# Attention's first two pairs in the written order, and the split parts of x stored a step earlier

## The chip, the cores and the metric

The kernel runs on one core of one Trainium2 chip. The metric is the device time in microseconds; before the change it is 2102.82 us, the median of 3 runs (2101.58 to 2103.69).

## What is computed

Three layers follow each other, all in float32:

```python
# attention: q, k, v of shape (4, 8, 576, 64)
scores = where(causal, -1e9, q @ k.T / 8)
local = softmax(scores) @ v
q_p = phi(q)                        # elu(q) + 1
mem_out = (q_p @ M_prev) / (q_p @ z_prev + 1e-6)
x = g * mem_out + (1 - g) * local   # g = sigmoid(beta), one per head
# x becomes (2304, 512)
x = (silu(x @ w_gate) * (x @ w_val)) @ w_out          # d_ff 1536
# routed layer, 8 experts, F 1024, all of them for every token
P = exp(logits - max); 8 times: rows, then columns to a sum of one, then * N / E
out = sum over e of P[:, e] * (relu(x @ w1[e]) @ w2[e])
```

## The kernel before

Products of float32 numbers are made of a high and a low part of each operand (names ending in H and L, or two halves of one tile), in three products; the low part is the difference between the number and its rounded high part. ACT makes the high part by a cast, DVE or POOL the low one by a subtraction.

**Attention** takes the 32 heads as 16 pairs. A pair's work is cut into steps by generators, and each has a letter: L loads a pair and makes its operands QH, QL, KH and KL (L301), Q prepares phi (ph, pz and nb, L333), S and E are scores (L396), N and K the factors from the row sums and the scaling on POOL (L372), V and Y the transposes (L474), W and U the products with the values (L515), C early weight work (L593), and X are filler matmuls into a spare PSUM tile (`po<-mask`), which give no result. Scores go by row blocks 4 (576 columns, in two halves), 3 (448), 2 (320, with block 0) and 1 (192). For each, PE writes a PSUM tile ps (there are two), DVE takes the row maximum (nm4 down to nm0), and ACT the exponent into P4 down to P1 and E0, with its sum. Then DVE turns the sums and the gate factors gs into factors, POOL scales P in place, PE transposes it into pt (three PSUM buffers), ACT and DVE copy it out (T, F, Z), and PE multiplies by the values into po, which is added up in xacc.

The strings BEGIN, ORDER and END (L39 to 57) give the order in which the steps are written: BEGIN the first two pairs, ORDER each later pair, shifted by the numbers in LAG, END what is left. The class `Ordered` (L79) hands every instruction to the scheduler with the demand to keep program order while `self.steady` is true. Before the change this is so only behind the steps of BEGIN and the first round of ORDER; the scheduler places what these steps issue freely on each engine. `gates` (L274) makes from beta eb, g1 and the ten small copies gs, and the high and low part of the routing weights (wgs). FIRST is the number of the step at which its second half is issued.

**The gated layer** (moe1) runs over 2304 tokens and **the routed layer** (moe2) over units of experts. The finished x is also needed as sums and differences of its blocks, in high and low parts, which are kept in DRAM. `parts_of` (L718) makes these: for each of a list of blocks a cast into a tile xl (two buffers), the difference, and a store xp<-xl. It is a generator, moved on by one step between pieces of the layers' own work; at each step it first does what is left from the step before, so a cast, its difference and its store fall into three following steps. Pairs 0 and 1 of token groups go through it in moe1 and pair 2 there too, with stores on SP's queue; pair 3 and the rest go through it in the first unit of moe2, with stores on ACT's queue. `logits` (L683) makes the routing logits in chunks and is moved on in the same way beside moe2's first unit; for a chunk of two tiles it has one step less in each of four rounds than for a larger one.

Of the kernel before, what the change touches and what calls it, by code (L numbers as in the profile page):

```python
# [42 lines left out]
ORDER = """  # L43
# [4 lines left out]


BEGIN = """  # L50
    L0 L0 Q0 X33 L1 L0 L0 S0 L2 X5 Q0 S0 S0 X5 S0 X7 X9 Q0 Q0 L1 Q1 L1 K0 X7 L1 S0 X5 Q1 N0 Q0 X7 X7 Q1
    V0 S0 S1 Q1 S1 S1 N0 V0 V0 V0 V0 V0 S1 S1 L2 Q1 L2 V0 W0 N0 W0 V0 V0 V0 S1 L2 V0 N1 N1 N1 W0
"""
END = """
# [1 line left out]
    U-1 U-1 U-1 U-1 U-1 U-1 U-1  # L56
"""

FIRST = 6

COPIES = "AAAAVVAVAVA"

# [1 line left out]
def schedule(n):  # L64

    steps = lambda text, base: [(s[0], base + int(s[1:])) for s in text.split()]
    middle = [(s, i + LAG[s]) for i in range(2, n) for s in ORDER.split() if i + LAG[s] < n]
    return steps(BEGIN, 0) + middle + steps(END, n)


def joined(steps, *counts):

    for n in counts:
        for _ in range(n):
            next(steps)
        yield
# [58 lines left out]
def f32(ap):  # L135
    return ap.bitcast(F32)
# [26 lines left out]
class Kernel:  # L163
# [34 lines left out]
    def attention(self, after=None):  # L198
        tc = self.tc
        nc = self.nc = Ordered(tc.nc, tc, lambda: self.steady)  # L200
        with ExitStack() as st, ExitStack() as first:
            pool = lambda n, b, to=st, **k: to.enter_context(tc.tile_pool(name=n, bufs=b, reuse_waits="tile", **k))

            self.s1, self.s2 = (pool(f"s{n}", n, first, side="right") for n in (1, 2))
            self.a1, self.a2, self.a3, self.a4 = (pool(f"a{n}", n) for n in (1, 2, 3, 4))
            self.pss = pool("pss", 2, space=PSUM)
            self.pst = pool("pst", 3, space=PSUM)
            self.pso = pool("pso", 1, space=PSUM)
            a1 = self.a1
            self.identb = self.s1.tile([P, P], BF16, name="identb")  # L210
            nc.vector.tensor_copy(self.identb, self.ident)

            self.mask = self.s1.tile([P, P], BF16, name="mask")
            nc.gpsimd.memset(self.mask, 0.0)
            nc.gpsimd.affine_select(
                out=self.mask, in_=self.mask, compare_op=ALU.is_ge, fill=MASKED,
                base=0, pattern=[[1, P]], channel_multiplier=-1,
            )
            self.mask0 = self.s1.tile([P, 2, 64], BF16, name="mask0")
            nc.gpsimd.memset(self.mask0, 0.0)  # L220
            for j in range(2):
                self.masked = nc.vector.tensor_copy(self.mask0[0:64, j], self.mask[0:64, 0:64])
            busy = self.pso.tile([P, 512], F32, name="po")

            self.P0 = []
            for n in range(2):
                t = a1.tile([P, 2, D], F32, name=f"P0{n}")
                nc.vector.memset(t, 0.0)
                self.P0.append(t)

            pairs = [(b, hp) for b in range(B) for hp in range(NP)][:self.n_pairs]
            n = len(pairs)
            live = [dict(b=b, hp=hp, P0=self.P0[hp % 2]) for b, hp in pairs]
            early = self.early()
            for p in live:
                p["steps"] = {
                    "L": self.load(p), "Q": self.prepare(p), "S": self.scores(p), "N": self.normalize(p),
                    "V": self.transposed(p), "W": self.values(p),
                }
                if p in live[:2]:  # L240
                    p["steps"]["S"] = joined(p["steps"]["S"], 2, 1, 2, 2, 2)
                if p is live[0]:
                    p["steps"]["V"] = joined(p["steps"]["V"], *10 * [1], 2)
                p["steps"].update({k: p["steps"][v] for k, v in SAME.items()})
                p["steps"]["C"] = early
            done = object()
            steps = schedule(n)
            for nth, (step, at) in enumerate(steps):
                self.steady = len(BEGIN.split()) + len(ORDER.split()) <= nth
                if nth == len(steps) - len(END.split()) and after:  # L250
                    self.ahead = self.load_units()
                    next(self.ahead)
                if nth == 1:
                    gates = self.gates()
                    next(gates)
                if nth == FIRST:
                    with tc.issue_after(self.low_q.ins):
                        next(gates, None)
                if step == "X":
                    for _ in range(at):  # L260
                        nc.tensor.matmul(busy[:, 0:P], self.mask, self.mask, start=True, stop=True)
                else:
                    next(live[at]["steps"][step], done)
            self.nc, self.steady = tc.nc, False
            first.close()
            if after:
                self.open_early(after)

                with tc.issue_after(self.last_exp.ins):
                    for _ in range(2):  # L270
                        next(self.ahead)
                    self.xs = self.split_x(*CHUNKS1[0])
# [410 lines left out]
    def logits(self, psum, name, pool, first, last, two=None):  # L683

        nc, m = self.nc, last - first
        pl = psum.tile([P, 512], F32, name=name)
        for k in range(NK):
            src = self.x[:, k, first * P:last * P]
            if two:
                t = [pool.tile([P, 512], F32R, name=two)[:, 0:m * P] for _ in range(2)]  # L690
            else:
                t = pool.tile([P, 2, 512], F32R, name="xl")
                t = [t[:, a, 0:m * P] for a in range(2)]
            nc.scalar.copy(t[0], src)
            if not two:
                yield
            nc.vector.tensor_sub(t[1], src, f32(t[0]))
            yield
            if two and m > 2:
                yield  # L700
            for a in range(2):
                nc.tensor.matmul(
                    pl[0:2 * E, 0:m * P], self.wgs[:, k], t[a], start=k + a == 0, stop=k == NK - 1 and a == 1
                )
        lt = pool.tile([P, 512], F32, name=two) if two else f32(pool.tile([P, 2, 512], F32R, name="xl")[:, 0])
        lt = lt[0:2 * E]
        nc.vector.tensor_copy(lt[:, 0:m * P], pl[0:2 * E, 0:m * P])
        yield
        yield
        pl = psum.tile([P, 512], F32, name=name)  # L710
        for t in range(m):
            nc.tensor.transpose(pl[:, t * 2 * E:(t + 1) * 2 * E], lt[:, t * P:(t + 1) * P], self.ident[0:2 * E, 0:2 * E])
        sums = self.Pw[:, first:last]
        pl = pl[:, 0:m * 2 * E].rearrange("p (t a e) -> p t a e", a=2, e=E)
        nc.vector.tensor_copy(sums, pl[:, :, 0])
        nc.vector.tensor_add(sums, sums, pl[:, :, 1])

    def parts_of(self, todo, queue):  # L718


        nc, rest = self.nc, []
        for src, dst in [*todo, (None, None), (None, None)]:
            nxt = []
            for what in rest:
                nxt += what()
            rest = nxt
            if src is not None:
                src = src()
                t = self.xl.tile([P, 2, 512], F32R, name="xl")
                hi, lo = (t[:, n].rearrange("p (k t) -> p k t", k=2) for n in range(2))  # L730
                nc.scalar.copy(hi, src)

                def low(src=src, dst=dst, t=t, hi=hi, lo=lo):
                    nc.vector.tensor_sub(lo, src, f32(hi))

                    def store():
                        queue.dma_start(dst, f32(t))
                        return []

                    return [store]  # L740

                rest.append(low)
            yield

    def parts(self, pair, queue):
# [22 lines left out]
    def moe1(self, last):  # L768
# [3 lines left out]
        with ExitStack() as st, ExitStack() as waiting, ExitStack() as banks:  # L772
# [61 lines left out]
            def more(c, logits):  # L834
                t0, n = CHUNKS1[c]
                if logits:
                    yield from self.logits(pgv, "p0", self.xl, t0 // P, (t0 + n) // P)
                yield from self.parts(c, nc.sync)
# [798 lines left out]
```

## Time and profile before

| | |
|---|---|
| median of 3 runs | 2102.82 us (2101.58 to 2103.69) |
| the profiled execution | 2105.53 us, span 2103.7 us |
| busy shares of the span | PE 98%, PEld 91%, DVE 82%, ACT 46%, POOL 25% |
| attention | from the start to about 230 us |

The profiled execution lies 2.7 us above the median. PE is TensorE's matmuls, PEld its weight loads, which overlap them. In attention nearly all instructions are recorded with one line, that of the wrapper (L93), so they are told apart by the tiles that they write and read; the names come without buffer numbers and without the block number, so P4 to P1 are all P, and the width tells them apart (576, 448, 320, 192).

### The profile page before, as it was taken

Reading aid. Unit: us, or ns where it says so; the run is one execution under the profiler, and the core shown is the slowest. Engines: PE = TensorE matmul, PEld = TensorE weight load, DVE = VectorE, ACT = ScalarE, POOL = GpSimd, SP = SyncE. Lnnn points to the kernel's source line nnn. Section 1 sums busy time; section 2 is a strip of 40 time slices with the busy share of each in tenths; the row PEclk is TensorE's granted clock in tenths of the full one; section 3 lists DMA queues with packets and bytes.
Section 4 is the critical chain, followed back from the end, with each engine's and each line's share of the span. In section 5 each row is a group of like instructions: output and inputs, shape, how many; then the busy total and the mean of one; then the engine's idle time right before and its main releaser. Section 6 shows DMA issues by size and latency. Waiting matters only on the chain.

```text
span 2103.7 us, 40585 instructions
## 1 busy us (share of the span) xinstructions
PE 2067.0 (98%) x15848; PEld 1907.4 (91%) x15848; DVE 1716.7 (82%) x3193; ACT 974.1 (46%) x1912; POOL 521.4 (25%) x458
## 2 busy tenths in 40 slices
PE   7999999999999999999999999999999999999999
PEld 5666787877889889999999999999999999999998
DVE  7899899675454668898888888888889888898887
ACT  6999543443333324444434444444444444444432
POOL 6888544000000042122121221212212122121210
PEclk9999999999999999999999999999999999999999
DMA  5342587476587747656566564665647656575564
GB/s 191 111 142 85 186 288 260 142 251 209 170 285 275 271 130 250 209 172 241 167 236 212 169 234 166 232 201 191 230 163 241 204 186 231 167 240 203 183 212 159
DMA packets 123359, 425.77 MB, mean 202 GB/s; under 512 B 13600, under 2 KB 13600, under 8 KB 120096
## 3 DMA queue, kind: packets, MB, share of 16 engines
q1 hardware_dynamic: 121728, 417.93, 59.3%
q10 hardware_dynamic: 1440, 5.24, 0.6%
q8 instruction: 126, 2.06, 0.4%
q14 instruction: 65, 0.53, 0.1%
HBM read 374.36 MB, written 48.76 MB: 201 GB/s over the span
## 4 chain that ended last, share of the span: by engine, by line
PE 71%; DVE 8%; DMA 4%; issue 1%; ACT 1%; SPq 0%; DVEq 0%; ACTq 0%
PE pu L1447 16%; PE pc L1284 15%; PE pq L1447 11%; PE pt L1284 10%; PE po L559 5%; PE pt L1370 4%; PE p L559 3%; PE pc L559 3%; PE pq L559 2%; DMA xr<-xp 2%; PE pt L559 2%; DMA xp<-xl 2%; DVE m L1300 2%; DVE xacc L1453 2%; DVE h L1269 1%; DVE h L1266 1%
## 5 line engine op out<-in xcount | busy, mean ns | idle before, releaser
L1447 PE MATMUL pu<-xl,h 128*128 128x256 f32 x3240 | 424.7, 278 | 2.6 <-DVE xacc L1453 2.1
L1447 PEld LDWEIGHTS pu<-xl,h 128*128 128x128 f32 x3240 | 393.0, 188 | 6.9 <-DVE xacc L1453 3.8
L1284 PE MATMUL pc<-xr,w 128*128 128x256 f32 x3048 | 390.5, 277 | 3.9 <-DMA xr<-xp 3.8
L1284 PEld LDWEIGHTS pc<-xr,w 128*128 128x128 f32 x3048 | 367.3, 188 | 7.2 <-issue 4.4
L1447 PE MATMUL pq<-xl,h 128*128 128x256 f32 x2430 | 317.1, 277 | 0.0
L1447 PEld LDWEIGHTS pq<-xl,h 128*128 128x128 f32 x2430 | 294.1, 188 | 0.4
L1284 PE MATMUL pt<-xr,w 128*128 128x256 f32 x2280 | 291.0, 277 | 0.0
L1268 ACT CAST h<-m 128x512 fp32r<-128x512 f32 (+1 forms) x345 | 190.4, 556 | 200.8 <-DVE m L1300 193.1
L1284 PEld LDWEIGHTS pt<-xr,w 128*128 128x128 f32 x2280 | 274.2, 188 | 0.7
L1453 DVE SCALAR_TENSOR_TENSOR xacc<-pu,Pw,xacc 128x256 f32<-128x256 f32 x540 | 237.1, 475 | 39.3 <-PE pu L1447 39.1
L1291 ACT COPY m<-pc 128x512 f32<-128x512 f32 x192 | 111.9, 583 | 249.6 <-PE pc L1284 245.7
L1453 DVE SCALAR_TENSOR_TENSOR xacc<-pq,Pw,xacc 128x256 f32<-128x256 f32 x405 | 177.5, 474 | 47.0 <-PE pq L1447 47.0
L1269 DVE TENSOR_TENSOR h<-m,h 128x512 fp32r<-128x512 f32 (+1 forms) x345 | 207.4, 625 | 1.5
L1189 POOL TENSOR_TENSOR ws<-raw 128x512 f32<-128x512 f32 x60 | 80.8, 1356 | 507.8 <-DMA raw<-w 165.6
L1265 ACT ACTIVATE h<-m 128x512 fp32r<-128x512 f32 x192 | 121.4, 633 | 172.3 <-DVE m L1296 164.9
L1300 DVE SCALAR_TENSOR_TENSOR m<-m 128x512 f32<-128x512 f32 x240 | 185.5, 773 | 14.2 <-ACT m L1327 10.6
L1296 DVE TENSOR_TENSOR m<-pt,m 128x512 f32<-128x512 f32 x192 | 131.3, 684 | 53.0 <-ACT m L1291 52.2
L559 PE MATMUL p<-xs,gw 128*128 128x512 f32 (+1 forms) x864 | 171.1, 355 | 3.4 <-ACT hf L796 1.3
L559 PEld LDWEIGHTS p<-xs,gw 128*128 128x128 f32 x864 | 142.3, 188 | 30.7 <-DVE hf L797 2.8
L1266 DVE SCALAR_TENSOR_TENSOR h<-m,h 128x512 fp32r<-128x512 f32 x192 | 150.3, 783 | 12.1 <-ACT h L1265 11.7
L1176 POOL TENSOR_TENSOR w<-raw,w 128x512 fp32r<-128x512 f32 x15 | 38.8, 2584 | 428.9 <-ACT w L1175 428.9
L559 PE MATMUL po<-h,ws 128*128 128x512 f32 x576 | 144.4, 391 | 0.2 <-DVE h L817 0.2
(232 smaller groups left out, 2956.9 us busy)
## 6 DMA issues: line engine op xcount, KB each, us to landing
xr<-xp SPq DMA_DIRECT2D x476, 512.0 KB, 4.2
raw<-w SPq DMA_DIRECT2D x64, 512.0 KB, 7.4
gw<-kg SPq DMA_DIRECT2D x24, 1024.0 KB, 7.0
graw<-gvo SPq DMA_DIRECT2D x36, 512.0 KB, 4.4
kg<-gw SPq DMA_DIRECT2D x24, 512.0 KB, 4.2
ws<-ko SPq DMA_DIRECT2D x24, 512.0 KB, 3.9
xp<-xl SPq DMA_DIRECT2D x21, 512.0 KB, 5.2
qk<-qkv SPq DMA_DIRECT2D x16, 640.0 KB, 5.2
```

The lines of the kernel that those rows point to most:

```text
L559: self.nc.tensor.matmul(out, lhs[a], rhs[b], start=start and n == 0, stop=stop and n == 2, skip_group_check=shared)
L1265: nc.scalar.activation(hi, src, AF.Relu)
L1266: self.later(1, lambda: nc.vector.scalar_tensor_tensor(lo, src, 0.0, f32(hi), op0=ALU.max, op1=ALU.subtract))
L1268: nc.scalar.copy(hi, src)
L1269: self.later(1, lambda: nc.vector.tensor_sub(lo, src, f32(hi)))
L1284: self.marks[3] = nc.tensor.matmul(out[:, j * HT:(j + 1) * HT], w[:, a, j, k], x[:, b, k], start=start and j + k + n == 0, stop=k + n == 3 ...
L1291: self.marks[1] = nc.scalar.copy(t, src)
L1296: nc.vector.tensor_add(t, a, b)
L1300: relu = lambda out, a, b, op: nc.vector.scalar_tensor_tensor(out, a, 0.0, b, op0=ALU.max, op1=op)
L1370: nc.tensor.matmul(ph[:, j * HT:(j + 1) * HT], w[:, b, j, k], x[:, c, k], start=j + a + k + m == 0, stop=a + k + m == 4, skip_group_check= ...
L1447: nc.tensor.matmul(po[:, c], h[a][:, x, j, c * P:(c + 1) * P], w2[b][:, y, j], start=start and c + j + n == 0, stop=j + n == 3, skip_group ...
L1453: self.marks[2] = nc.vector.scalar_tensor_tensor(acc, po[:, c], self.Pw[:, at, e:e + 1], acc, op0=ALU.mult, op1=ALU.add)
```

## The change

Four things are edited. All steps of attention are kept in program order (`self.steady` is always true). The first run of fillers has 12 instead of 33. The second half of `gates` is issued at step 18 instead of 6. In `parts_of` the difference is issued with the cast, in the same step, and the store a step later, so that a block takes two steps instead of three and the list ends a step earlier; and `logits` has the extra step in each round for every chunk.

```diff
--- before.py
+++ after.py
@@ -48,7 +48,7 @@
 
 
 BEGIN = """
-    L0 L0 Q0 X33 L1 L0 L0 S0 L2 X5 Q0 S0 S0 X5 S0 X7 X9 Q0 Q0 L1 Q1 L1 K0 X7 L1 S0 X5 Q1 N0 Q0 X7 X7 Q1
+    L0 L0 Q0 X12 L1 L0 L0 S0 L2 X5 Q0 S0 S0 X5 S0 X7 X9 Q0 Q0 L1 Q1 L1 K0 X7 L1 S0 X5 Q1 N0 Q0 X7 X7 Q1
     V0 S0 S1 Q1 S1 S1 N0 V0 V0 V0 V0 V0 S1 S1 L2 Q1 L2 V0 W0 N0 W0 V0 V0 V0 S1 L2 V0 N1 N1 N1 W0
 """
 END = """
@@ -56,7 +56,7 @@
     U-1 U-1 U-1 U-1 U-1 U-1 U-1
 """
 
-FIRST = 6
+FIRST = 18
 
 COPIES = "AAAAVVAVAVA"
 
@@ -245,8 +245,9 @@
                 p["steps"]["C"] = early
             done = object()
             steps = schedule(n)
+            self.steady = True
             for nth, (step, at) in enumerate(steps):
-                self.steady = len(BEGIN.split()) + len(ORDER.split()) <= nth
+                self.steady = True
                 if nth == len(steps) - len(END.split()) and after:
                     self.ahead = self.load_units()
                     next(self.ahead)
@@ -696,7 +697,7 @@
                 yield
             nc.vector.tensor_sub(t[1], src, f32(t[0]))
             yield
-            if two and m > 2:
+            if two:
                 yield
             for a in range(2):
                 nc.tensor.matmul(
@@ -719,7 +720,7 @@
 
 
         nc, rest = self.nc, []
-        for src, dst in [*todo, (None, None), (None, None)]:
+        for src, dst in [*todo, (None, None)]:
             nxt = []
             for what in rest:
                 nxt += what()
@@ -730,16 +731,13 @@
                 hi, lo = (t[:, n].rearrange("p (k t) -> p k t", k=2) for n in range(2))
                 nc.scalar.copy(hi, src)
 
-                def low(src=src, dst=dst, t=t, hi=hi, lo=lo):
-                    nc.vector.tensor_sub(lo, src, f32(hi))
-
-                    def store():
-                        queue.dma_start(dst, f32(t))
-                        return []
-
-                    return [store]
-
-                rest.append(low)
+                nc.vector.tensor_sub(lo, src, f32(hi))
+
+                def store(dst=dst, t=t):
+                    queue.dma_start(dst, f32(t))
+                    return []
+
+                rest.append(store)
             yield
 
     def parts(self, pair, queue):
```

On DVE, in the first pair (rows from the first reduces of pair 0 on; ps is the scores' tile): before, the gs copies come first.

```order
L93 TENSOR_REDUCE nb_333<-pz_331 128x10
L93 COPY gs_222<-g1_218 64x4
L93 COPY gs_222<-g1_218 128x4 x4
L93 COPY gs_222<-g1_218 64x4
L93 COPY gs_222<-g1_218 128x4 x4
L93 TENSOR_REDUCE nm4_256<-ps_240 128x1
L93 TENSOR_REDUCE nm4_258<-ps_241 128x1
L93 SCALAR_TENSOR_TENSOR ph_342<-zq_212,ph_342 128x640
L93 SCALAR_TENSOR_TENSOR nb_333<-nb_333,eb_215 128x10
L93 TENSOR_TENSOR pz_399<-ph_342,zq_212 128x640
L93 RECIPROCAL nb_333<-nb_333 128x10
L93 TENSOR_REDUCE nm3_283<-ps_274 128x2
```

Now the reduces of pair 0 come right behind its low part QL, and eb, g1 and gs behind nm2.

```order
L93 TENSOR_REDUCE nm4_215<-ps_199 128x1
L93 TENSOR_REDUCE nm4_217<-ps_200 128x1
L93 SCALAR_TENSOR_TENSOR ph_172<-zq_159,ph_172 128x640
L93 TENSOR_REDUCE nm3_242<-ps_233 128x2
L93 TENSOR_REDUCE nm0_266<-ps_252 128x1
L93 TENSOR_REDUCE nm2_261<-ps_252 128x2
L93 TENSOR_TENSOR pz_290<-ph_172,zq_159 128x640
L93 TENSOR_SCALAR eb_292<-eb_292 128x8
L93 RECIPROCAL g1_295<-eb_292 128x8
L93 TENSOR_SCALAR g1_295<-g1_295 128x8
L93 RECIPROCAL g1_295<-g1_295 128x8
L93 COPY gs_299<-g1_295 64x4
```

The gs copies moved from ahead of the first reduce to behind five reduces; behind them now come wgs, nb, QL of pair 1 and two steps on sums, and then nm1 of pair 0.

On ACT, from the operands of pair 2 (QH_519, KH_521) or from P4 of pair 1 on: before (P1_371 is of pair 0, P4_413, P3_449 and P2_500 of pair 1).

```order
L93 ACTIVATE QH_519<-qk_261 128x640
L93 CAST KH_521<-qk_261 128x640
L93 ACTIVATE P1_371,sums_238<-ps_360,nm1_369 128x192 x2
L93 COPY T_404<-pt_406 128x4x128
L93 COPY T_405<-pt_456 128x4x128
L93 ACTIVATE P4_413,sums_412<-ps_414,nm4_430 128x576
L93 CAST F_402<-pt_462 128x512
L93 ACTIVATE P4_413,sums_412<-ps_415,nm4_432 128x576
L93 COPY T_404<-pt_469 128x3x128
L93 COPY T_405<-pt_474 128x3x128
L93 ACTIVATE P3_449,sums_412<-ps_438,nm3_447 128x448 x2
L93 ACTIVATE P2_500,sums_412<-ps_483,nm2_492 128x320 x2
```

After (P4_392, P3_428, P2_479 and P1_495 are of pair 1, QH_498 and KH_500 of pair 2).

```order
L93 ACTIVATE P4_392,sums_391<-ps_393,nm4_409 128x576
L93 ACTIVATE P4_392,sums_391<-ps_394,nm4_411 128x576
L93 ACTIVATE P3_428,sums_391<-ps_417,nm3_426 128x448 x2
L93 COPY T_384<-pt_435 128x4x128
L93 CAST F_381<-pt_441 128x512
L93 COPY T_383<-pt_448 128x3x128
L93 COPY T_384<-pt_453 128x3x128
L93 ACTIVATE P2_479,sums_391<-ps_462,nm2_471 128x320 x2
L93 ACTIVATE E0_482,sums_391<-ps_462,nm0_476 128x64
L93 ACTIVATE P1_495,sums_391<-ps_484,nm1_493 128x192 x2
L93 ACTIVATE QH_498<-qk_220 128x640
L93 CAST KH_500<-qk_220 128x640
```

QH and KH of pair 2 moved from ahead of pair 0's P1 to behind pair 1's P1, and the copies T, F, T, T from between and ahead of the exponents to between P3 and P2.

On POOL, from the first scaling of pair 0 on (KL_522 before and KL_501 after are of pair 2; ph_342 and ph_321 of pair 1): before.

```order
L93 TENSOR_TENSOR ph_172<-ph_172,nb_333 128x640
L93 TENSOR_SCALAR P4_239<-P4_239,sums_238 128x576 x2
L93 TENSOR_SCALAR P3_285<-P3_285,sums_238 128x448 x2
L93 TENSOR_TENSOR ph_342<-ph_342,nb_435 128x640
L93 TENSOR_TENSOR KL_522<-qk_261,KH_521 128x640
L93 TENSOR_SCALAR P2_310<-P2_310,sums_238 128x320 x2
L93 TENSOR_SCALAR P00_151<-E0_313,sums_238 64x64 x2
L93 TENSOR_SCALAR P1_371<-P1_371,sums_238 128x192 x2
L93 TENSOR_SCALAR P4_413<-P4_413,sums_412 128x576 x2
```

After.

```order
L93 TENSOR_SCALAR P3_244<-P3_244,sums_197 128x448 x2
L93 TENSOR_TENSOR ph_172<-ph_172,nb_312 128x640
L93 TENSOR_SCALAR P2_269<-P2_269,sums_197 128x320 x2
L93 TENSOR_TENSOR KL_501<-qk_220,KH_500 128x640
L93 TENSOR_TENSOR ph_321<-ph_321,nb_414 128x640
L93 TENSOR_SCALAR P00_151<-E0_272,sums_197 64x64 x2
L93 TENSOR_SCALAR P1_350<-P1_350,sums_197 128x192 x2
L93 TENSOR_SCALAR vmr_536<-vm_222 128x256
L93 TENSOR_TENSOR vmr_536<-vm_222,vmr_536 128x256
```

Before, P2 and P00 stood between KL of pair 2 and P1 of pair 0, and ph of pair 1 ahead of that KL; now ph of pair 1 and P00 stand between them, and the KL itself can run only when KH of pair 2, now behind pair 1's P1 on ACT, is there.

## Rows read from the trace of the kernel before

**Rows 1.** The page: busy time by engine; chain that ended last, share by engine.

```profile
PE 2067.0 (98%) x15848; PEld 1907.4 (91%) x15848; DVE 1716.7 (82%) x3193; ACT 974.1 (46%) x1912; POOL 521.4 (25%) x458
...
PE 71%; DVE 8%; DMA 4%; issue 1%; ACT 1%; SPq 0%; DVEq 0%; ACTq 0%
```

**Rows 2.** Windows: us, busy of PE, PEld, DVE, ACT, POOL; PEclk, DMA, GB/s.

```profile
9.20:15.75 6.55, 4.82 (x61) 4.28 (x59) 5.90 (x19) 3.59 (x7) 3.72 (x5) 1.00 0.93 351
20.00:25.00 5.00, 5.00 (x37) 4.30 (x36) 2.96 (x9) 4.21 (x13) 2.99 (x6) 0.51 0.87 345
60.00:85.40 25.40, 24.82 (x197) 17.16 (x196) 20.88 (x45) 24.14 (x69) 23.13 (x31) 1.00 0.39 114
```

**Rows 3.** Timeline, start: start, us, engine, line, operation, tiles [idle before].

```profile
7.10 3.70 PE L93 MATMUL po<-mask 128*128 128x128 bf16 x33
...
13.54 2.32 DVE L93 COPY gs<-g 64x4 f32<-64x4 f32 x10
...
15.77 1.41 DVE L93 TENSOR_REDUCE nm<-ps 128x1 f32<-128x576 f32 x2
...
16.55 0.74 ACT L93 ACTIVATE P<-ps,nm 128x576 f32<-128x576 f32 x1 [2.40 <-DVE nm L93]
...
17.43 0.47 PE L93 MATMUL ps<-KH,QH 64*128 64x448 f32 x2 [3.42 <-ACT P L93]
...
19.88 0.64 ACT L93 ACTIVATE P<-ps,nm 128x448 f32<-128x448 f32 x1 [1.77 <-DVE nm L93]
...
21.89 0.53 ACT L93 ACTIVATE P<-ps,nm 128x320 f32<-128x320 f32 x1 [0.67 <-DVE sums L93]
...
23.43 0.74 ACT L93 ACTIVATE QH<-qk 128x640 fp32r<-128x640 f32 x1
...
24.69 0.41 ACT L93 ACTIVATE P<-ps,nm 128x192 f32<-128x192 f32 x1
```

**Rows 4.** Timeline 26 to 53 us, of POOL, PE and ACT.

```profile
26.69 1.55 POOL L93 TENSOR_TENSOR KL<-qk,KH 128x640 fp32r<-128x640 f32 x1
...
29.60 0.72 POOL L93 TENSOR_SCALAR P<-E,sums 64x64 f32<-64x64 f32 x2
30.41 0.82 POOL L93 TENSOR_SCALAR P<-P,sums 128x192 f32<-128x192 f32 x2
...
43.40 1.26 POOL L93 TENSOR_TENSOR ph<-ph,nb 128x640 f32<-128x640 f32 x1 [0.36 <-DVE nb L93]
...
30.20 0.41 PE L93 MATMUL ps<-KH,QH 64*128 64x320 f32 x2
...
36.32 0.41 PE L93 MATMUL ps<-KH,QH 64*128 64x288 f32 x2
...
28.09 0.59 ACT L93 CAST F<-pt 128x512 fp32r<-128x512 f32 x1 [0.27 <-PE pt L93]
...
30.75 0.63 ACT L93 ACTIVATE P<-ps,nm 128x448 f32<-128x448 f32 x1
...
32.57 0.53 ACT L93 ACTIVATE P<-ps,nm 128x320 f32<-128x320 f32 x1 [0.48 <-DVE nm L93]
...
33.88 0.74 ACT L93 ACTIVATE QH<-qk 128x640 fp32r<-128x640 f32 x1
...
39.33 0.74 ACT L93 ACTIVATE P<-ps,nm 128x576 f32<-128x576 f32 x1 [0.84 <-DVE nm L93]
...
40.77 0.58 ACT L93 COPY xacc<-po 128x512 f32<-128x512 f32 x1
```

**Rows 5.** Waits of PE from 425 to 720 us: total, times, longest.

```profile
PE pc L559 <- ACT hf L1076: 2.5, 2, 1.6
PE pu L712 <- DVE m L707: 1.7, 1, 1.7
PE pu L702 <- ACT m L694: 1.2, 1, 1.2
```

**Rows 6.** Waits of ACT from 425 to 720 us.

```profile
ACT xl L731 <- DMA xp<-xl: 19.6, 12, 3.8
```

## The prediction

> **What bounds the kernel now.** I read the page first: PE is busy 98% of the span and carries 71% of the chain that ended last, DVE 8% [rows 1]. So TensorE's stream is the kernel, and a change counts by the idle time of PE that it makes or removes. In attention's even part, between 60 and 85.4 us, PE is busy 24.82 of 25.40 us [rows 2]: two pairs have 0.58 us to give. What is lost at the start therefore stays lost. Only the start itself, up to pair 2, has slack, and there I read the timeline engine by engine.
>
> There the reader sees three things [rows 3]. The 33 fillers take 3.70 us and hold PE until 10.80. DVE's ten gs copies (13.54, 2.32 us) stand ahead of the first two reduces (15.77), so the first exponent, P4 of pair 0, begins at 16.55 after 2.40 us of waiting for them, and PE's next scores wait 3.42 us for P4. After that ACT does pair 2's QH at 23.43, ahead of pair 0's P1 at 24.69: the freely placed order takes the operands of pair 2 very early.
>
> For the stores of x's parts I read the waits of ACT and PE between 425 and 720 us. ACT's cast waits 19.6 us in 12 times for a store to land and free one of two buffers [rows 6]; PE's own waits behind that are 2.5, 1.7 and 1.2 us [rows 5].
>
> **The start, step by step.** The sum is made against the profiled execution, 2105.53 us, which is 2.7 us above the median 2102.82.
>
> *The lead.* Twelve fillers at 3.70/33 = 0.11 us take 1.35 us, so scores of pair 0 begin near 8.45 instead of 10.7. No gs copy stands ahead of the reduces any more. From the start of a group's scores to its exponent takes 2.4 us where nothing is in between (30.20 to 32.57 [rows 4]), so P4 of pair 0 begins near 10.9: 5.7 us earlier. P3 follows 3.33 later (16.55 to 19.88), P2 after another 2.01 [rows 3], near 16.2, and E0 ends 1.31 behind P2's start (32.57 to 33.88 [rows 4]), near 17.5.
>
> *Where it goes.* eb, the four small steps on g1, the gs copies, wgs, pz, nb and QL of pair 1 are not gone; they now stand between nm2 and nm1 of pair 0 on DVE, and eb's exponent stands behind E0 on ACT. In the old order one stretch from 9.20 to 15.75 held this work and ph of pair 0, 19 records, 5.90 us busy [rows 2]. ph is now ahead, two short steps on sums join: about 5.5 to 6 us from 17.7 on. nm1 then starts near 23.4 and P1 of pair 0 near 24.2, against 24.69. Of 5.7 us of lead 0.5 is left. Behind nm1 DVE still has ph, nb and pz of pair 1 ahead of the reduces nm4, and pair 1's scores need the buffer that P1 frees. I take P3 of pair 1 as level with 30.75 [rows 4]; it could be 0.5 ahead. It could also be 2.5 behind: in 20 to 25 us PE was busy all 5.00 us at a granted clock of 0.51 [rows 2], so that stretch at full clock would have been 2.5 shorter, and if pair 1's scores fall into such a stretch they cost that.
>
> *What is late next.* In the new order ACT has P3 of pair 1, then T, F, T, T, and only then P2; PE has five groups of transposes ahead of the 320 scores, and the fifth needs the buffer that F's cast frees. So: P3 at 30.75, two exponents of 0.63, T and F at 0.59 each [rows 4] make 33.2; the scores to P2 take 2.4; P2 begins near 35.6 instead of 32.57. E0 is over 1.31 later (36.9) and two P1 of 0.41 bring QH of pair 2 to 37.7, instead of 23.43 [rows 3]. QH and KH, 0.74 each by that row, end at 39.2, and POOL's KL (1.55) at 40.7. On POOL this KL now stands ahead of ph of pair 1 (1.26), P0 (0.72) and P1 (0.82) of pair 0 [rows 4], so P1 is scaled at 43.5. PE's transposes of that P1 and the values that use them stand ahead of pair 2's scores. Those transposes and their copies cost at least two copies of 0.59: scores of pair 2 near 44.7. From scores to the copy of xacc took 4.45 (36.32 to 40.77 [rows 4]); in the new order this copy and two ph exponents of QH's size (0.58 + 1.48) stand ahead of P4 of pair 2 on ACT. All in series gives 51.2, against 39.33: **+12**. Some steps overlap (the first half of P1, the 0.1 us by which records on ACT overlap, the remaining 0.5 of the lead): I take **+10**, with ends +8 and +12. The rest of attention has the same order on every engine as before, so the lag lasts; what 13 more pairs could give back at 0.29 us each is 3.8 us, were all idle time of PE filled, which nothing here does.
>
> *The loads.* In the new order SP issues the early raw weights behind zq of pair 2, which now waits for pair 0's pz. Their first use comes with pair 2's steps, which are late themselves: nothing. Were that cover gone, the price would again be a wait of pair 2, inside the ends above.
>
> **Parts and routing.** Each of the 30 stores is issued a step earlier, ahead of the next cast on ACT or past a weight load on SP, so a cast that waits for the buffer waits less. The waits of PE in this stretch sum to 5.4 us [rows 5], the most that can be gained. Against it, DVE's difference stands directly behind the cast: when ACT waits, DVE's other work (h, m, xacc) queues behind the difference. Two more waits of the size of m's 1.7 would lose 3. Nearest is the gain side, since the waits of 1.7 and 1.2 lie behind such casts, and I take **−3**. The four extra steps of routing issue no instruction; they end routing four steps later, before the second unit needs Pw: nothing, and a wait like the 1.2 above if not.
>
> **Sum:** 2105.5 + 10 − 3 = 2112.5 profiled, less 2.7: **2110 us**. Its own range, by the ends, is 2105 to 2115.
>
> **Rivals.** About 4.2 us (0.2%) can be told from no change.
>
> *The lead survives (faster).* If P1 of pair 0 and so pair 1 come off DVE early, the 5.7 us last through pair 2 and with the stores make 2102.8 − 5.7 − 3 = 2094. For it: the reduces and P4 do come 5.7 earlier. Against it: 5.5 us or more of DVE work between nm2 and nm1. It decides at nm1: it would have to start before about 19.
>
> *Level start.* Pair 2's late operands are hidden by work of pair 1, and only the stores count: 2100. For it: P3 of pair 1 is level, and PE has transposes and values of two pairs to do. Against: these stand behind the same P1 and copies.
>
> *The stores do not help.* They leave a step earlier, yet land no earlier where it matters (the queue is busy), or DVE is held up behind the casts: the change then does not do what it says there. 2113 to 2116.
>
> *TensorE's clock.* In 20 to 25 us the granted clock was 0.51, the 1.2 GHz level, after PE had waited 3.42 us before 17.43 [rows 2, 3]. In the new order PE has its last 19 fillers behind the scores for nm1, at 0.11 us each some 2 us, and then waits until sums and POOL have scaled P4, near 24; that is a wait of the same size, and it would meet pair 1's scores: 2.5 us more than forecast, 2112.5. The Trainium skill says this too ("TensorE: Matmul & The Clock Gate", section "HAM oscillation — how this bites in real kernels"): work that follows a long enough idle gap of TensorE starts at the low clock again. By that rule the removed fillers are themselves a cost, and the trace's fall to 0.51 agrees.
>
> **Chances.** Forecast 0.50; stores do not help 0.12; clock 0.08; level 0.17; lead survives 0.13. The range takes in the level start and the worst of the stores: 2099 to 2116; the surviving lead lies outside it. Faster by over 0.2%: 0.13. Within 0.2%: 0.20, the level start and the low end of the forecast. Slower: 0.67.
>
> **What would show it.** Right: P4 of pair 0 near 11, P1 of pair 0 still near 24, P3 of pair 1 near 31, QH of pair 2 near 38, P4 of pair 2 near 50, and the same distance for P4 of later pairs; ACT's wait for stores below 19.6 us and PE's waits for hf and m mostly gone. Wrong: QH of pair 2 before 33, or P4 of pair 2 before 44; then the start is level or better. If the lag is there but the time is not, later stretches give it back, and the pairs' distance would show where.

## The result: 2122.29 us, 0.85% slower

The changed kernel takes 2122.29 us (median of 5 runs, 2121.48 to 2125.76) against 2103.69 us of the kernel before in the same rounds. The ratio is 1.0085, with a 95% interval of 1.0069 to 1.0102: some 18 us slower, between 14.5 and 21.5. The direction was forecast, the size was not: 2110 was given, and 2116 as the upper end. The profiled execution took 2121.53 us (span 2119.7), 16.0 more than that of before.

The page first: the kernel still is PE's stream, as in [rows 1], and PE's busy time has hardly changed.

```profile
PE 2068.8 (98%) x15827; PEld 1907.3 (90%) x15827; DVE 1715.3 (81%) x3193; ACT 974.3 (46%) x1912; POOL 524.1 (25%) x458
...
PE 71%; DVE 7%; DMA 4%; issue 1%; ACT 0%; SPq 0%; DVEq 0%; ACTq 0%
```

To see where the 16 us are, both spans are cut at the same four places of the program: the end of attention's last product into po, the gated layer's last product into po, the first weighting by Pw (L1453, near the end of the first unit of the routed layer), and the end. The columns are those of [rows 2]. The kernel before:

```profile
0.00:227.60 227.60, 210.70 (x1654) 147.53 (x1655) 190.93 (x395) 195.75 (x546) 184.27 (x242) 0.99 0.41 129
227.60:670.40 442.80, 436.69 (x2103) 360.02 (x2102) 307.85 (x519) 171.68 (x293) 67.08 (x33) 1.00 0.70 235
670.40:796.70 126.30, 121.95 (x795) 108.51 (x794) 85.33 (x174) 43.78 (x79) 27.97 (x29) 0.97 0.62 208
796.70:2103.70 1307.00, 1297.67 (x11304) 1291.39 (x11302) 1132.55 (x2108) 562.84 (x995) 242.13 (x154) 1.00 0.60 203
```

And after:

```profile
0.00:243.10 243.10, 213.10 (x1633) 148.02 (x1634) 190.08 (x395) 196.13 (x546) 184.26 (x243) 0.96 0.39 121
243.10:683.20 440.10, 435.96 (x2103) 360.14 (x2102) 307.09 (x520) 171.44 (x294) 67.44 (x33) 1.00 0.71 237
683.20:812.60 129.40, 120.60 (x794) 106.73 (x793) 87.11 (x173) 43.75 (x79) 27.51 (x29) 1.00 0.60 201
812.60:2119.70 1307.10, 1299.13 (x11304) 1292.38 (x11302) 1131.05 (x2108) 562.93 (x995) 244.89 (x154) 1.00 0.61 204
```

Attention takes 243.1 instead of 227.6 us (+15.5), the gated layer 440.1 instead of 442.8 (−2.7), the first unit 129.4 instead of 126.3 (+3.1), and the rest is level (+0.1). The gated layer's share should not be read closely: with its code unchanged it took from 439.7 to 444.3 us in the profiles of the experiments below. In attention PE is idle for 30.0 us instead of 16.9 (span of the window less PE's busy time), and busy 2.4 us more although 21 fillers are gone: part of its work ran at the lower clock.

The timeline of ACT at the start answers to [rows 3] and [rows 4], step by step:

```profile
10.69 0.74 ACT L93 ACTIVATE P<-ps,nm 128x576 f32<-128x576 f32 x1 [2.24 <-DVE nm L93]
...
16.88 0.53 ACT L93 ACTIVATE P<-ps,nm 128x320 f32<-128x320 f32 x1 [0.98 <-DVE nm L93]
...
23.93 0.42 ACT L93 ACTIVATE P<-ps,nm 128x192 f32<-128x192 f32 x1 [2.76 <-DVE nm L93]
...
32.12 0.64 ACT L93 ACTIVATE P<-ps,nm 128x448 f32<-128x448 f32 x1 [2.31 <-DVE nm L93]
...
37.65 0.53 ACT L93 ACTIVATE P<-ps,nm 128x320 f32<-128x320 f32 x1 [2.46 <-DVE nm L93]
...
39.75 0.75 ACT L93 ACTIVATE QH<-qk 128x640 fp32r<-128x640 f32 x1
...
53.20 0.59 ACT L93 COPY xacc<-po 128x512 f32<-128x512 f32 x1 [5.17 <-PE po L93]
...
55.09 0.72 ACT L93 ACTIVATE P<-ps,nm 128x576 f32<-128x576 f32 x1
```

P4 of pair 0 begins at 10.69, 5.9 us ahead of before, as forecast. By P1 of pair 0 (23.93 against 24.69) all of that lead but 0.8 us is gone; the forecast left 0.5. P4 of pair 2 begins at 55.09 against 39.33: 15.8 us late. From there to the last pairs the distance stays between 15.3 and 15.8. What PE waits for in between shows in its own timeline and in POOL's:

```profile
24.35 1.11 PE L93 MATMUL pt<-ident,P 128*128 128x128 f32 x4 [5.49 <-POOL P L93]
...
45.24 1.09 PE L93 MATMUL pt<-ident,P 128*128 128x128 f32 x3 [6.66 <-POOL P L93]
...
48.39 0.61 PE L93 MATMUL ps<-KH,QH 64*128 64x288 f32 x2
```

```profile
41.20 1.55 POOL L93 TENSOR_TENSOR KL<-qk,KH 128x640 fp32r<-128x640 f32 x1 [7.67 <-ACT KH L93]
...
44.76 0.83 POOL L93 TENSOR_SCALAR P<-P,sums 128x192 f32<-128x192 f32 x2
```

PE waits 5.49 us until POOL has scaled P4 of pair 0, and 6.66 us until it has scaled P1 of pair 0, which stands behind KL of pair 2 there. Only then, behind the transposes and products that hang on this P1, come the scores of pair 2, at 48.39.

In the first unit PE's waits (from 683 to 813 us) are these; they answer to [rows 5]:

```profile
PE pc L1282 <- DMA xr<-xp: 4.0, 2, 2.1
PE pu L1132 <- DVE cs L1128: 3.6, 3, 1.5
PE pc L1282 <- DVE xacc L986: 0.9, 1, 0.9
```

The waits for m are gone, as forecast, and the wait for hf in the gated layer fell from 2.5 to 1.2 us. In their place PE waits 3.6 us for cs, the column sums of the routing's eight rounds, for which it did not wait before, and 4.0 us for parts of x that are read back (0.6 before). ACT's waits for stores went from 19.6 us [rows 6] to 13.9:

```profile
ACT xl L732 <- DMA xp<-xl: 13.9, 12, 2.3
```

### The profile page after: what moved, and what is told of

The parts are those of the page before. It is cut to its first block, busy times and chain, and to the rows that moved or that the text cites. A ratio compares the mean times of both kernels' runs of the same rounds, so it can differ in the third digit from the quotient of the medians.

```text
span 2119.7 us, 40535 instructions
## 1 busy us (share of the span) xinstructions
PE 2068.8 (98%) x15827; PEld 1907.3 (90%) x15827; DVE 1715.3 (81%) x3193; ACT 974.3 (46%) x1912; POOL 524.1 (25%) x458
## 4 chain that ended last, share of the span: by engine, by line
PE 71%; DVE 7%; DMA 4%; issue 1%; ACT 0%; SPq 0%; DVEq 0%; ACTq 0%
PE pu L1445 16%; PE pc L1282 15%; PE pq L1445 11%; PE pt L1282 11%; PE po L560 5%; PE pt L1368 4%; DMA xr<-xp 3%; PE p L560 3%; PE pc L560 3%; PE pq L560 2%; PE pt L560 2%; DVE xacc L1451 1%; DVE m L1298 1%; DMA xp<-xl 1%; DVE h L1267 1%
```

## Experiments

Each kernel was timed in rounds with the kernel before, and the ratios below are to it. One thousandth is 2.1 us.

| what is changed from the kernel before | ratio | 95% interval | us |
|---|---|---|---|
| the whole change | 1.0085 | 1.0069 to 1.0102 | +17.9 |
| start alone | 1.0074 | 1.0062 to 1.0086 | +15.6 |
| parts alone | 0.9984 | 0.9970 to 0.9998 | −3.4 |
| routing steps alone | 1.0040 | 1.0027 to 1.0054 | +8.4 |
| parts and routing | 1.0013 | 1.0003 to 1.0022 | +2.7 |
| start and parts | 1.0070 | 1.0055 to 1.0085 | +14.7 |
| program order alone | 1.0073 | 1.0053 to 1.0093 | +15.4 |

### The four parts of the change

**Start alone.** The edit, on the kernel before:

```diff
-    L0 L0 Q0 X33 L1 L0 L0 S0
+    L0 L0 Q0 X12 L1 L0 L0 S0
-FIRST = 6
+FIRST = 18
-                self.steady = len(BEGIN.split()) + len(ORDER.split()) <= nth
+                self.steady = True
```

> Only the start of the change (program order for all of attention, 12 fillers instead of 33, the gates' second half at step 18); parts and routing as before. Theory: the start alone makes the loss, P4 of pair 2 near 55.1 as in the changed kernel (39.3 before), and 2103 + 15.5 = about 2118.5, some 3 under or level with the changed kernel. Rival: the start costs the 10 forecast and the rest comes from the parts: about 2113.

Measured: 2118.80 us, ratio 1.0074. P4 of pair 2 begins at 56.50, against 55.09 in the changed kernel. The start carries the loss; the theory stands, and the 10 us of the forecast are too few.

**Parts alone.** The hunk of `parts_of` in the diff, and nothing else.

> Only the cast and difference in one step and the store a step earlier; start and routing as before. Theory: it takes PE's waits for hf and m in the gated layer and the first unit and gains 3 to 4 us: about 2100. Rival: what the earlier stores gain they lose again in waits of PE for parts read back (those grew from 0.6 to 4.2 us in the first unit of the changed kernel): 2103, no change.

Measured: 2097.62 us, ratio 0.9984: the 3 us that were forecast. PE's waits in the first unit, in this kernel (676 to 798 us):

```profile
PE pc L1281 <- DVE xacc L985: 0.9, 1, 0.9
PE pc L1281 <- DMA xr<-xp: 0.5, 1, 0.5
PE pu L702 <- DVE m L697: 0.3, 1, 0.3
```

The waits of 1.7 and 1.2 us for m are down to 0.3. The waits for hf are not: they are 4.8 us in the gated layer, against 2.5 before. The gain is therefore seen in the first unit only, 121.0 us against 126.3. This is the version that beats both kernels, by little. The profiled execution took 2106.06 us, 8.4 above the median, so its gated layer (444.7 us) does not show what the stores do there; the start alone, with the old stores, has 439.7 us, so the 2.7 us that the whole change shows there cannot be put down to the stores either.

**Parts and routing**, and **the changed kernel less the routing steps**. The edits:

```diff
-            if two and m > 2:
+            if two:
```

added to parts alone, and taken back from the changed kernel.

> Parts and the four extra routing steps; start as before. Theory: the extra steps push the eight rounds of row and column sums into a place where PE waits for cs (3.6 us in the changed kernel, none before), so the gain of the parts is lost: 2103 to 2104. Rival: the extra steps cost nothing and this run is as fast as parts alone: 2100.

> The changed kernel with the routing steps as before. Theory: PE's waits for cs are gone, 2122 - 3 = about 2119. Rival: the waits for cs come from the lag and the parts, not from the extra steps: 2122, no difference to the changed kernel.

Measured: 2105.47 us (1.0013) and 2117.15 us (1.0070). With the old start the extra steps cost 6 us on top of the parts (1.0013 against 0.9984), with the new one about 3 (1.0085 against 1.0070; these two intervals overlap). Without them the changed kernel has no wait for cs in its first unit. In parts and routing PE waits for cs again, from 671 to 800 us:

```profile
PE pu L1131 <- DVE cs L1127: 4.2, 3, 1.5
PE pc L1281 <- DMA xr<-xp: 1.9, 1, 1.9
PE pc L1281 <- ACT h L1262: 1.1, 1, 1.1
```

**Routing alone** and **parts with no extra step at all**. The edits are the line above on the kernel before; and, on parts alone:

```diff
-            if two and m > 2:
-                yield
```

> The kernel before with nothing but the four extra routing steps. Theory: they alone bring PE's waits for cs in the first unit and cost 3 to 6 us: 2107. Rival: they cost only together with the earlier stores: 2103.

> Parts alone, with the extra routing step in no chunk at all (the other way round). Theory: the loss of the extra steps is where the row and column sums fall among PE's work, so ending them earlier keeps them clear of it: as parts alone or better, 2095 to 2098. Rival: the steps space PE's routing products from the casts and differences they wait for, and without them PE waits: 2100 to 2105.

Measured: 2109.10 us (1.0040) and 2103.85 us (1.0012; 1.0000 to 1.0023). So four steps that issue nothing cost 8.4 us by themselves, more than theory gave, and fewer steps are no gain either: against parts alone they lose some 6 us. The first unit of routing alone, 669 to 802 us:

```profile
PE pu L702 <- ACT m L694: 2.8, 1, 2.8
PE pu L1134 <- DVE cs L1130: 2.4, 2, 1.5
PE pt L1284 <- DMA xr<-xp: 2.1, 1, 2.1
PE pu L712 <- DVE m L707: 0.9, 1, 0.9
PE pc L1284 <- DMA xr<-xp: 0.9, 1, 0.9
```

These five rows make 9.1 us, against 3.5 for m and the parts in the kernel before, where there was no wait for cs; of the two waits for m one is longer and one shorter. With fewer steps there is no cs row, and PE waits 3.2 us for parts read back instead. The length of the first unit says the same: 124.2 to 127.9 us in the ten profiles with the old stores and steps, 121.0 and 123.8 with the new stores alone, 128.7 and 129.4 with the stores and the extra steps, 132.2 with the extra steps alone, and 126.4 with the stores and fewer steps. The steps decide beside which of PE's products the sums fall; why just these places wait was not taken further, and no run separates the three kinds of wait.

### The start, taken apart

**Program order alone** (33 fillers, gates at step 6, only `self.steady` is true) and **gates at step 6** (the start alone with FIRST = 6).

> Program order for all of attention, but 33 fillers and the gates' second half at step 6 as before; parts and routing as before. Theory: the written order of the first two pairs is what costs, through the late operands of pair 2 and the P1 of pair 0 behind them; fewer fillers and late gates only move the beginning: P4 of pair 2 at 54 to 57 again, about 2117. Rival: the order alone costs little, the late gates and missing fillers make the loss: below 2107, P4 of pair 2 under 44.

> The start alone, with the gates' second half at step 6 again. Theory: the 3 us of small DVE steps go back ahead of the first reduce, where they cost the lead of P4 of pair 0 (near 14 instead of 10.7), and no longer stand between nm2 and nm1; P1 of pair 0 comes at about the same time, 23 to 24, so the place of the gates is worth 0 to 1 us: 2118. Rival: the late gates are the cause of the loss: under 2110.

Measured: 2121.56 us (1.0073) and 2118.41 us (1.0060; 1.0041 to 1.0080). P4 of pair 2 begins at 54.83 and 54.53. The rival of the late gates falls, and so does that of the fillers: between these two kernels only the first fillers differ, P4 of pair 0 begins at 11.84 in both, and their intervals overlap. The program order makes the loss. With the gates early in program order that is 1.2 us later than in the changed kernel, not the 3 that were expected.

**P1 scaled first.** One step of the list is moved:

```diff
-    V0 S0 S1 Q1 S1 S1 N0 V0 V0 V0 V0 V0 S1 S1 L2 Q1 L2 V0 W0 N0 W0
+    V0 S0 S1 Q1 S1 S1 N0 V0 V0 V0 V0 V0 S1 S1 N0 L2 Q1 L2 V0 W0 W0
```

> The start alone, with one step of the written list moved: the scaling of P0 and P1 of pair 0 on POOL stands ahead of the making of KL of pair 2, not behind it. Theory: PE's wait of 5 to 6.7 us for that P1 near 45 us is gone, PE goes on from its transposes to where it needs KL of pair 2 itself (ready near 42.8), and P4 of pair 2 comes 3 to 5 us earlier than with the start alone: 2118.8 - 4 = about 2115. Rival: PE waits as long for KL of pair 2 itself and nothing is gained: 2118.

Measured: 2115.95 us, ratio 1.0045 (1.0028 to 1.0061), about 6 us better than the start alone, a little more than expected. PE no longer waits there, pair 2's scores come at 44.25 (49.23 in the start alone) and its P4 at 51.31 (56.50):

```profile
41.73 0.48 PE L93 MATMUL pt<-ident,P 128*128 128x128 f32 x1 [0.60 <-ACT T L93]
...
43.20 1.12 PE L93 MATMUL po<-T,vm 128*64 128x256 f32 x4
44.25 0.61 PE L93 MATMUL ps<-KH,QH 64*128 64x288 f32 x2
```

**Fillers in the gaps.**

```diff
-    ... N0 Q0 X7 X7 Q1
+    ... N0 Q0 X40 X40 Q1
-    ... L2 Q1 L2 V0 W0 N0 W0 V0 V0 V0
+    ... L2 Q1 L2 V0 W0 N0 W0 Z90 V0 V0 V0
```

where Z is fillers into a tile pt.

> The start alone, with 66 fillers more behind the scores for nm1 and 90 fillers where PE waits for P1 of pair 0. The order of all other work is the same. Theory: TensorE's granted clock stays up from 24 to 55 us (0.50 there with the start alone), and the work of pair 1 and pair 2 that ran at the low clock on the path is shorter: 3 to 6 us gained, about 2114. Rival: the path there is DVE, ACT and POOL, and the low clock is hidden: 2118.

Measured: 2116.85 us, ratio 1.0060 (1.0038 to 1.0082): 3 us better than the start alone by the ratios, the lower end of what was expected, and the intervals overlap. The clock did what it was to do in the second gap only: in the first the fillers ended 1.81 us before the transposes, which still took 0.66 us, but the scores behind them ran at the low clock. P4 of pair 2 comes at 52.61, against 56.50 in the start alone and 55.09 in the changed kernel. Windows of the start alone, the last columns being granted clock, DMA share and GB/s:

```profile
25.00:30.00 5.00, 3.39 (x21) 2.43 (x20) 3.28 (x5) 2.14 (x5) 4.59 (x6) 0.50 0.78 306
30.00:35.00 5.00, 4.25 (x20) 3.14 (x18) 2.04 (x4) 3.04 (x8) 1.04 (x2) 0.50 0.00 0
35.00:40.00 5.00, 5.00 (x27) 3.70 (x25) 2.23 (x6) 1.62 (x8) 0.00 (x0) 0.50 0.01 2
40.00:45.00 5.00, 0.96 (x5) 0.30 (x4) 1.16 (x2) 1.97 (x6) 2.95 (x3) 0.50 0.15 21
45.00:50.00 5.00, 3.91 (x18) 2.60 (x20) 1.32 (x6) 1.48 (x5) 2.38 (x7) 0.50 0.28 112
```

With the fillers:

```profile
25.00:30.00 5.00, 3.39 (x24) 2.27 (x24) 3.40 (x6) 2.14 (x5) 4.72 (x6) 0.54 0.85 332
30.00:35.00 5.00, 3.80 (x24) 3.10 (x22) 2.41 (x5) 3.06 (x8) 1.04 (x2) 0.78 0.00 1
35.00:40.00 5.00, 5.00 (x41) 3.64 (x38) 2.06 (x7) 3.07 (x12) 0.00 (x0) 0.66 0.02 7
40.00:45.00 5.00, 4.82 (x81) 4.45 (x79) 0.97 (x2) 0.50 (x2) 4.34 (x7) 1.00 0.34 114
45.00:50.00 5.00, 5.00 (x38) 3.01 (x39) 2.80 (x9) 1.27 (x5) 3.22 (x6) 1.00 0.05 21
```

From the transposes of pair 0's P1 to the scores of pair 2, with the fillers:

```profile
44.52 0.84 PE L93 MATMUL pt<-ident,P 128*128 128x128 f32 x3
...
46.42 0.40 PE L93 MATMUL ps<-KH,QH 64*128 64x288 f32 x2
```

That is 1.90 us at a granted clock of 1.00; the same work in the same order took 3.15 us (45.24 to 48.39) in the changed kernel, at 0.50.

**Pair 1's scores first**, and **the mended order** with everything together:

```diff
-    V0 S0 S1 Q1 S1 S1 N0 V0 V0 V0 V0 V0 S1 S1 L2 Q1 L2 V0 W0 N0 W0
+    V0 S0 S1 Q1 S1 S1 N0 S1 V0 V0 V0 V0 V0 S1 L2 Q1 L2 V0 W0 N0 W0
```

```diff
-    ... N0 Q0 X7 X7 Q1
+    ... N0 Q0 X40 X40 Q1
-    V0 S0 S1 Q1 S1 S1 N0 V0 V0 V0 V0 V0 S1 S1 L2 Q1 L2 V0 W0 N0 W0
+    V0 S0 S1 Q1 S1 S1 N0 N0 L2 S1 V0 V0 V0 V0 V0 S1 Q1 L2 V0 W0 W0
```

> The start alone, with the step that makes pair 1's 320 scores, its P2 and E0, moved ahead of pair 0's transposes in the written list. Theory: the copies T, F, T, T on ACT and five groups of transposes on PE no longer stand between P3 and P2 of pair 1; P2 of pair 1 begins near 34 to 35 instead of 37.7 and QH of pair 2 near 37.5 instead of 39.8, a gain of 2 to 3 us: 2116. Rival: the copies and transposes are only moved behind P2, P1 of pair 1 waits for them, and QH of pair 2 comes as late as before: 2118.

> The start alone with all that the runs pointed to: P0 and P1 of pair 0 scaled ahead of KL of pair 2, pair 2's QH, KH and KL made ahead of pair 1's P2, pair 1's 320 scores ahead of pair 0's transposes, and 66 fillers more behind the scores for nm1. Theory: the written order loses by these places and by the low clock, each apart, so the loss of 15.5 us falls to 2 to 5: 2105 to 2108, P4 of pair 2 at 43 to 46. Rival: the loss is in the long DVE work ahead of nm1 and cannot be moved: 2114, as with P1 first alone.

Measured: 2115.71 us (1.0068; 1.0055 to 1.0082) and 2110.62 us (1.0049; 1.0034 to 1.0063). The first is a miss: its median is near the 2116 expected, but by the ratios, which compare with the kernel before in the same rounds, it gains 1.3 us on the start alone and not 2 to 3, and the intervals overlap. P2 of pair 1 did come early, at 33.62, but P1 of pair 1 only at 38.30, behind the copies that had been passed, and QH of pair 2 at 39.10 (39.75 in the changed kernel, 40.61 in the start alone). The rival's words fit better. The mended order brings P4 of pair 2 to 48.83, 6 us earlier than the changed kernel, but not to the 43 to 46 expected, and by the ratios it is no better than P1 first alone (1.0049 against 1.0045), which is what its rival said. Single gains do not add up here; what takes them back, DVE's work ahead of nm1 as the rival has it or another place, no run shows. The mended order does show one thing clearly. Its fillers stand ahead of pair 1's scores, the granted clock is 1.00 from 24.28 to 26.10, and P3 of pair 1 comes at 30.79, where the forecast had it (30.75), and not at 32.12:

```profile
30.79 0.64 ACT L93 ACTIVATE P<-ps,nm 128x448 f32<-128x448 f32 x1 [2.31 <-DVE nm L93]
```

**The list or the round behind it.** Free again is only the first round of ORDER, or only the list of the first two pairs:

```diff
-                self.steady = True
+                self.steady = not len(BEGIN.split()) <= nth < len(BEGIN.split()) + len(ORDER.split())
```

```diff
-                self.steady = True
+                self.steady = len(BEGIN.split()) <= nth
```

> The start alone, but the first round behind the first two pairs' list is again left to the scheduler, which then puts the two ph exponents and P4 of pair 2 ahead of the copy of xacc on ACT and frees DVE likewise; the list of the first two pairs stays in its written order. Theory: of the loss of 15.5 us some 4 to 5 belong to this round (with the mended list P4 of pair 2 still came at 48.8, behind xacc at 46.9): 2113 to 2115. Rival: all of it belongs to the first two pairs' list: 2118.

> The start alone, but the first two pairs' list is left to the scheduler as before, and only the round behind it is in written order. QH of pair 2 is ahead of P1 of pair 0 again. Theory: the list of the first two pairs carries 10 of the 15.5 us, so this is 2106 to 2108, with P4 of pair 2 near 43. Rival: the round alone delays pair 2 as much: over 2112.

Measured: 2117.64 us (1.0069; 1.0054 to 1.0084) and 2107.55 us (1.0020; 1.0009 to 1.0030). The theory for the first falls: freeing the round alone gives back about 1 us by the ratios, and the intervals overlap. The second came as expected. ACT with the list left free:

```profile
20.11 0.75 ACT L93 ACTIVATE QH<-qk 128x640 fp32r<-128x640 f32 x1
...
23.07 0.43 ACT L93 ACTIVATE P<-ps,nm 128x192 f32<-128x192 f32 x1
...
43.04 0.72 ACT L93 ACTIVATE P<-ps,nm 128x576 f32<-128x576 f32 x1
```

QH of pair 2 is at 20.11, ahead of P1 of pair 0, and P4 of pair 2 at 43.04. Of 15.5 us some 11 hang on the written list of the first two pairs; the remaining 4 are there with the round in written order, 12 fillers and the late gates, and these three were not taken apart with the list free.

## Why the prediction was wrong

**The mechanism was right.** The lead of P4 (10.9 forecast, 10.69 measured), its use by DVE's work between nm2 and nm1 (P1 of pair 0 at 24.2, 23.93), QH of pair 2 behind pair 1's P1, KL of pair 2 ahead of P1 of pair 0 on POOL, pair 2's scores behind that P1, the copy of xacc and two ph ahead of P4: all stand in the trace, in this order. The lag lasted (15.3 to 15.8 us to the last pairs), as argued from PE's 24.82 busy us of 25.40 [rows 2]. The rivals of a surviving lead and of a level start are out.

**The step that failed is PE's part in "All in series gives 51.2 ... Some steps overlap: I take +10".** P4 came at 55.09, 15.8 us late: the 2 us taken off for overlap were not there (PE began 0.35 us before POOL had ended with P1, little more), and the series was itself too short by 3.9. By its terms:

| step | forecast | measured | added here |
|---|---|---|---|
| P3 of pair 1 | 30.75 | 32.12 | 1.4 |
| P2 of pair 1 | 35.6 | 37.65 | 0.7 |
| QH of pair 2 | 37.7 | 39.75 | 0.0 |
| P1 of pair 0 scaled, its end | 43.5 | 45.6 | 0.0 |
| scores of pair 2 | 44.7 | 48.39 | 1.6 |
| copy of xacc | 49.15 | 53.20 | 0.4 |
| P4 of pair 2 | 51.2 | 55.09 | −0.2 |

The durations on ACT and POOL taken from [rows 3, 4] held within a tenth or two. What was under-sized is PE's part. Where the forecast put two copies of 0.59 us between P1 of pair 0 and the scores of pair 2, PE had three groups of transposes and a group of four products to do, 45.24 to 48.39, at a granted clock of 0.50; with fillers ahead of them they took 1.90 us and not 3.15, so 1.25 of the 1.6 are the clock. The same holds for P3 of pair 1, "level with 30.75" in the sum: its pair's scores ran behind the wait of 5.49 us, again at 0.50 (24.35 to 27.50), and where fillers kept the clock up it came at 30.79. From the scores of pair 2 to the copy of xacc it was 4.81 us, and 4.30 with the fillers. So some 3 of the 3.9 us are the low clock, an estimate from single profiles. The 0.7 at P2 is another thing: ahead of its scores PE waited 1.03 and 0.41 us for the copies T.

The clock was in the prediction, as 2.5 us by which P3 could be late and as a rival with a chance of 0.08, both outside the sum; it was part of the likeliest case instead, since both long waits that the new order makes for PE were followed by the low clock (four transposes took 1.11 us at 24.35 in the profile after, and 0.66 at 24.28 in the mended order, where fillers stand ahead of them). The rival's own wait was too small as well: the 19 fillers took 1.22 us and not some 2, and PE then waited 5.49 us and not 3.4. A long stall was priced by the instructions that it delays at their durations behind a busy PE, not at those behind an idle one. The time of the fillers experiment gives the same size, about 3 us by the ratios, though its interval overlaps that of the start alone. By the rule of the Trainium skill that the prediction named ("TensorE: Matmul & The Clock Gate", section "HAM oscillation — how this bites in real kernels"), work behind a long enough idle gap starts at the low clock, and the trace agrees: 0.50 behind the waits of 5.49 and 6.66 us.

**The other step that failed is "The four extra steps of routing issue no instruction ... nothing", with "a wait like the 1.2 above if not".** Alone they cost 8.4 us (5.7 to 11.3), beside the parts about 6, and in the whole change about 3. The cover that was named, that Pw is needed only by the second unit, holds for the end of the routing, but the eight rounds in between have products on PE, which wait for DVE (cs): 3.6 us in the changed kernel and 4.2 beside the parts. Why the new places are worse than the old stays open.

**Parts: right.** −3 was taken, from the waits for m, and −3.4 (−6.3 to −0.4) was measured alone, with those waits down from 2.9 to 0.3 us; the waits for hf, which were also to go, did not go there. On top of the new start it shows less (1.0070 with, 1.0074 without), and these two cannot be told apart. A loss from DVE held up behind ACT's casts does not show in parts alone: in the first unit PE waits 0.9 us for DVE's xacc, as before, and 0.3 for its m.

**The sum**, with measured terms: start +15.6, parts −3.4, routing +3 to +8.4 makes +15 to +21 against 17.9 measured; the forecast had +10, −3 and 0.

## What to carry to other kernels

Where a scheduler has placed the start of a pipeline well, forcing the written order there fixes whatever the list happens to say: look first at which operands of the next stage end up behind the last work of this one, and which in-order queue (here POOL) then makes old work wait behind new. When such a chain is summed, add it in series and price TensorE's instructions behind each long wait (5.5 and 6.7 us here) at the low clock. A step that issues nothing still moves everything behind it (four of them cost 8.4 us here); price it by what it moves past, not by what it contains.

## What the runs showed that was not expected

The low clock can last far beyond the wait that brings it. In the start alone the granted clock was 0.50 in each 5 us from 25 to 50 (the windows above), with PE busy 4.25 and 5.00 us of 5 in two of them before the second long wait, which runs from 41 to 46; the changed kernel has the same order there, and its clock was 0.50 in 25 to 30, 0.75 in 30 to 35 and back at 1.00 in 35 to 40:

```profile
25.00:30.00 5.00, 3.39 (x21) 2.47 (x21) 3.37 (x6) 2.14 (x5) 4.72 (x6) 0.50 0.83 304
30.00:35.00 5.00, 3.55 (x21) 2.56 (x20) 1.89 (x4) 2.88 (x8) 1.04 (x2) 0.75 0.00 0
35.00:40.00 5.00, 3.58 (x31) 2.43 (x31) 2.29 (x7) 2.54 (x12) 0.00 (x0) 1.00 0.01 3
```

Attention took 246.3 and 243.1 us in these two profiles. A third of the same order, the changed kernel less the routing steps, is like the first: 0.50 in all five of those stretches and 246.2 us. So one and the same order can differ by 3 us with the clock, which is as much as some of the terms above; those sizes rest on the timed ratios where there are any, not on one profile. Why the clock came back in one of the three and not in the others is not shown.
